# Attention with sigmoid and two mixture layers on one core: the last 64 keys of a head as a fourth, overlapping block, some weight splits on DVE alone, other pacing costs and a warm-up

## The chip, the cores and the metric

The kernel runs on one core of a Trainium2 chip. The metric is the device time of one execution in microseconds (us). Of the engines, TensorE (PE in the profile; PEld is its weight loads) multiplies matrices into PSUM, VectorE (DVE) and ScalarE (ACT) work element by element, GpSimd (POOL) issues the indirect transfers, and SyncE (SP) issues the other DMAs. Each engine runs its instructions in the order of the program; semaphores make it wait for the others.

## The reference

There are three stages, over 4 batches, 12 heads, 448 positions and 64 features a head, thus 1792 tokens of 768 features:

```python
scores = scale * np.matmul(q, k.transpose(0, 1, 3, 2)) - np.log(S)
attn = 1.0 / (1.0 + np.exp(-scores))
out = np.matmul(attn, v)                           # stage 1
x = out.transpose(0, 2, 1, 3).reshape(B * S, H * D)
h = np.maximum(np.maximum(x @ w1, x @ w2), x @ w3)
x = h @ w_out                                      # stage 2
logits = x @ w_gate + modality_bias[modality_id]   # stage 3: 8 experts, the best one per token
out[mask] = gate_w[mask, None] * (np.maximum(x[mask] @ w1[e], 0.0) @ w2[e])
```

The attention is a sigmoid of each score by itself; there is no sum over keys to divide by. The four weights of stage 2 (`w1`, `w2`, `w3`, `w_out`) come as 64-bit floats.

## The kernel before, in words

Most matmuls use a fast form of fp32 (`fp32r`). To keep the precision, an operand is split into a rounded part and the rest (`split`, line 172: ScalarE copies the rounded part, DVE subtracts it), and a product is made of three matmuls: rounded by rounded, rounded by rest, rest by rounded. Attention times values is in plain fp32.

**Attention** (lines 309 to 370). A unit is a pair of heads; there are 24. For a unit, SP loads queries and keys (`load_qk`), and values (`load_v`), three or four units ahead; `split_qk` (line 250) makes the rounded part and the rest on ScalarE and DVE. `emit_qk` (line 266) makes the scores: 448 keys are three blocks of 128 and a rest of 64. A full block takes 6 matmuls (three products, two heads side by side on 64 rows each; line 276). The rests of both heads are put together in one 128x128 weight tile, `k2`, that POOL fills and in which the other entries stay zero (lines 262 and 323), so they take three full matmuls (line 279). Each block's scores go to one of three PSUM buffers in turn (line 270), and a sigmoid on ScalarE (line 284) moves them to SBUF. `emit_av` multiplies by the values: line 296 for a full block, line 299 for the rests, in two tiles of 64x64. `evac_X` (line 301) splits the result out of PSUM into `xR` and `xL`, on DVE alone.

The order of an iteration, by hand, is: scores and sigmoids of unit u+1 (behind its first block: the loads, and the split of unit u+2), attention times values of unit u, its evacuation, and then a piece of `background` work.

**Background work** (lines 212 to 238). The weights of stage 2 arrive in 24 chunks. A chunk takes one load on SP, six conversion steps on DVE (64-bit to 32-bit float, `cv_ops`, lines 161 to 169) and, for the 18 chunks that are not of `w_out`, a `split` into one of four places of a ring (lines 173 and 174). These are entries of a queue, `bg`, each with a cost in us that is written down by hand; `background(us)` takes entries until their written costs have used up the budget:

```python
while us > 0 and (bg or bg2):
    ...
    if bg and (bg[0][2] is None or bg[0][2] in used):
        op, cost, _ = bg.popleft()
    elif bg2 and loaded[0] > LAST_O and step[0] >= bg2[0][2]:
        op, cost, _ = bg2.popleft()
    else:
        return
    op()
    us -= cost
```

The first queue goes ahead; an entry that would overwrite a ring place still to be used blocks it, and then the second one, `bg2`, has its turn. In attention, from unit 3 on, the budget is 1.2 a unit, until the chunk (1, 0), the fourth of the ring, is ready.

**Projection** (lines 414 to 440). 36 calls of `project`, "projects" 0 to 35: six blocks of 128 features, two halves of the tokens, three weights. Each has 36 matmuls (line 423) into one of two PSUM buffers. The first weight's result is copied by ScalarE (line 427), and the other two are joined to it with a maximum on DVE (line 429). Behind each project stands a "slot", `background(5.4)`. Beside the chunks, the slots make the gate weights: the product of `w_out` and `w_gate` (`bg2`, lines 393 to 412), in three tables of 48 operations each on DVE (line 402). A table is asked for by a DMA (line 399), and its operations may come only two projects later. Line 407 sums up the three, and line 440 empties both queues behind the last slot.

**After it.** The logits (line 447) are made from the maxima and the gate weights, ahead of everything else on TensorE. Then `w_out` and the maxima are split (lines 459 to 472), and `layer2` (line 487) follows with the routing of the tokens beside it, and then the experts.

Of the kernel before, what the change touches and what calls it, by code (L numbers as in the profile page):

```python
# [23 lines left out]
E64_LO = float(np.uint32(0x38000000).view(np.float32))  # L24
E64_HI = float(np.uint32(0x47EFFFFF).view(np.float32))
# [3 lines left out]
def attn_moe_kernel(  # L29
# [15 lines left out]
    nc = tc.nc  # L45
    B, HP, D, _, _, S = qk.shape
# [3 lines left out]
    FB = FF // 128  # L50
    NU = B * HP
    NJ = S // 128
    NB = 2 * NJ + 1
    SR = S - 128 * NJ
    TT = NT // 128
    GT = 256
# [7 lines left out]
    XW = DM + 16  # L64
    qscale = 1.0 / float(D) ** 0.5
    ln_s = float(np.log(S))

# [5 lines left out]
    def hold(tag, name, *shape):  # L75
        return pool.tile([128, *shape], F32, tag=tag, name=name)

    def r(ap):
        return ap.bitcast(F32R)

    def cut(a, off, *shape):

        n = 1
        for s in shape:
            n *= s
        a = a[:, off:off + n]
        if len(shape) == 2:
            a = a.rearrange("p (a b) -> p a b", a=shape[0])
        elif len(shape) == 3:
            a = a.rearrange("p (a b c) -> p a b c", a=shape[0], b=shape[1])  # L90
        return a
# [5 lines left out]
    xR = [xR_[:, i] for i in range(KB)]  # L97
    xL = [xLa[:, i] for i in range(KB - 1)] + [xLb[:, 0]]

    at_ = hold("H1", "at", 2 * NB * S + NB * D)  # L100
    atb = [cut(at_, NB * S * i, NB, S) for i in range(2)]

    kq_ = hold("H2", "kq", 8 * S)
    kq = [cut(kq_, 4 * S * i, 2, 2, S) for i in range(2)]

    k2_ = hold("K1", "k2", 2, 2, 128)
    k2 = [k2_[:, i] for i in range(2)]
    u1, u2, u3 = (hold(f"U{i}", f"u{i}", 2048) for i in range(3))
    qk_in = [cut(u, 2 * S * i, 2, S) for u in (u1, u2) for i in range(2)]
    v_in = [cut(u3, NB * D * i, NB, D) for i in range(4)] + [cut(at_, 2 * NB * S, NB, D)]  # L110

    stage = [hold(f"S{i}", f"stage{i}", KB * 256).bitcast(I32) for i in range(2)]
    cv_ = hold("S2", "cv", 2, 768)
# [31 lines left out]
    def ps(tag, shape, name):  # L145
        return psum.tile(shape, F32, tag=tag, name=name)
# [5 lines left out]
        return psum.tile(shape, F32, tag=f"a{a_n[0]}", name=name)  # L152


    def cv_ops(i, dst):
        st = stage[i % 2].rearrange("p (n two) -> p n two", two=2)
        lo, hi = st[:, :, 0], st[:, :, 1]
        v1, v2 = cv1, cv2
        ve = nc.vector
        return [  # L160
            lambda: ve.tensor_scalar(out=v1.bitcast(I32), in0=hi, scalar1=0x7FFFFFFF, scalar2=None, op0=ALU.bitwise_and),
            lambda: ve.tensor_scalar(out=v1, in0=v1, scalar1=E64_LO, scalar2=E64_HI, op0=ALU.max, op1=ALU.min),
            lambda: ve.tensor_scalar(out=v1.bitcast(I32), in0=v1.bitcast(I32), scalar1=0x0FFFFFFF, scalar2=3,
                                     op0=ALU.bitwise_and, op1=ALU.logical_shift_left),
            lambda: ve.scalar_tensor_tensor(out=v1.bitcast(U32), in0=lo.bitcast(U32), scalar=29, in1=v1.bitcast(U32),
                                            op0=ALU.logical_shift_right, op1=ALU.bitwise_or),
            lambda: ve.tensor_scalar(out=v2.bitcast(U32), in0=hi.bitcast(U32), scalar1=-0x80000000, scalar2=0x40000000,
                                     op0=ALU.bitwise_and, op1=ALU.bitwise_xor),
            lambda: ve.tensor_tensor(out=dst().bitcast(U32), in0=v1.bitcast(U32), in1=v2.bitcast(U32), op=ALU.bitwise_xor),  # L169
        ]  # L170

    def split(dR, dL, src):
        nc.scalar.activation(out=r(dR), in_=src, func=ACTF.Copy)  # L173
        nc.vector.tensor_tensor(out=r(dL), in0=src, in1=dR, op=ALU.subtract)  # L174

    ws = [w.bitcast(I32) for w in (w1, w2, w3)]
# [6 lines left out]
    def flat(a):  # L183
        return a.rearrange("p a b -> p (a b)")
# [28 lines left out]
    for i, (kind, a, b) in enumerate(chunks):  # L213
        bg.append((load_chunk, 0.0, None))
        ops = cv_ops(i, (lambda: cv1) if kind == "w" else (lambda a=a: wof[a]))
        bg.extend((op, 0.65, None) for op in ops)
        if kind == "w":
            m = w_ring[ring_no[a, b]]
            old = [c for c in ring_no if ring_no[c] == ring_no[a, b] and c < (a, b)]
            bg.append((lambda m=m, c=(a, b): (split(flat(m[:, 0]), flat(m[:, 1]), cv1), ready.add(c)), 0.85,  # L220
                       old[-1] if old else None))
    bg2 = deque()
    step = [0]
    ready = set()
# [16 lines left out]
    def load_qk(u):  # L241
        b, hp = divmod(u, HP)
        for h in range(2):
            nc.sync.dma_start(out=qk_in[u % 4][D * h:D * (h + 1)], in_=qk[b, hp, :, h])

    def load_v(u):
        b, hp = divmod(u, HP)
        nc.sync.dma_start(out=v_in[u % 5], in_=v[b, hp])

    def split_qk(u):  # L250
        src, kt = qk_in[u % 4], kq[u % 2]
        if u == 0:
            nc.vector.tensor_copy(out=r(kt[:, 0, 0]), in_=src[:, 0])
            nc.scalar.activation(out=r(kt[:, 0, 1]), in_=src[:, 1], func=ACTF.Copy)  # L254
            for i in range(2):
                nc.vector.tensor_tensor(out=r(kt[:, 1, i]), in0=src[:, i], in1=kt[:, 0, i], op=ALU.subtract)
        else:
            nc.scalar.activation(out=r(kt[:, 0]), in_=src, func=ACTF.Copy)
            nc.vector.tensor_tensor(out=r(kt[:, 1]), in0=src, in1=kt[:, 0], op=ALU.subtract)
        for h in range(2):  # L260
            p = slice(D * h, D * (h + 1))
            nc.gpsimd.tensor_copy(out=r(k2[u % 2][p, :, SR * h:SR * (h + 1)]), in_=kt[p, :, 0, 128 * NJ:])

    s_n = [0]

    def emit_qk(u, g):


        kt = kq[u % 2]
        s = ps(("a0", "a1", "t")[s_n[0] % 3], [128, 2, 512], "s")  # L270
        s_n[0] += 1
        for n, (a, x) in enumerate(((0, 0), (0, 1), (1, 0))):
            if g < NJ:
                for h in range(2):
                    p = slice(D * h, D * (h + 1))
                    nc.tensor.matmul(s[:, h, 0:S], r(kt[p, a, 0, 128 * g:128 * (g + 1)]), r(kt[p, x, 1]),  # L276
                                     start=(n == 0), stop=(n == 2))
            else:
                nc.tensor.matmul(s[:, 0, 0:S], r(k2[u % 2][:, a]), r(kt[:, x, 1]), start=(n == 0), stop=(n == 2))  # L279
        return s  # L280

    def emit_sig(u, g, s):
        n = 2 if g < NJ else 1
        nc.scalar.activation(out=atb[u % 2][:, 2 * g:2 * g + n], in_=s[:, 0:n, 0:S],  # L284
                             func=ACTF.Sigmoid, scale=qscale, bias=nlns)

    X_t = {}
# [1 line left out]
    def emit_av(u, g):  # L289
        if g == 0:  # L290
            X_t[u] = ps(f"x{u % 2}", [128, 512], "X")
        vt, at = v_in[u % 5], atb[u % 2]
        for h in range(2):
            dst = X_t[u][64 * h:64 * h + 64, 0:S]
            if g < NJ:
                nc.tensor.matmul(dst, vt[:, 2 * g + h], at[:, 2 * g + h], start=(g == 0), stop=False)  # L296
            else:
                p = slice(SR * h, SR * (h + 1))
                nc.tensor.matmul(dst, vt[p, 2 * NJ], at[p, 2 * NJ], start=False, stop=True)  # L299

    def evac_X(u):
        b, hp = divmod(u, HP)
# [5 lines left out]

    with tc.manual_schedule(engines={mybir.EngineType.PE, mybir.EngineType.Activation, mybir.EngineType.DVE, SP}):
        load_qk(0)  # L310
        make_identity(nc, ident)
        nc.vector.memset(nlns, -ln_s)
        nc.scalar.activation(out=gate[:, 0:1], in_=nlns, func=ACTF.Sigmoid)
# [3 lines left out]
        load_v(1)  # L317
        load_qk(3)
        load_v(2)
        nc.vector.memset(gw, 0.0)  # L320
        nc.vector.memset(ones, 1.0)
        for i in range(2):
            nc.vector.tensor_copy(out=r(k2[i]), in_=gw.rearrange("p a b -> p (a b)")[:, 0:1].unsqueeze(1).to_broadcast([128, 2, 128]))

        nc.gpsimd.memset(tri, 1.0)
        nc.gpsimd.affine_select(out=tri, in_=tri, pattern=[[1, 128]], compare_op=ALU.is_gt, fill=0.0,
# [81 lines left out]

        for c in range(3):
            bg2.append((lambda c=c: gate_load(c), 0.0, 0))  # L410
            bg2.extend((lambda c=c, kb=kb, e=e: gate_op(c, kb, e), 0.47, 100 + c) for kb in range(KB) for e in range(E))
        bg2.append((gate_end, 0.2, 0))

        def project(fb, half, wi):
# [18 lines left out]
        for fb in range(KB):  # L433
            for half in range(2):
                for wi in range(3):
                    project(fb, half, wi)
                    step[0] += 1
                    background(5.4)
        step[0] += 100
        background(999)  # L440

# [526 lines left out]
```

## Time and profile before

| | |
|---|---|
| time, median of 3 runs | 806.4 us (804.61 to 807.2) |
| time of the profiled execution | 807.21 us |
| its span | 805.5 us |
| TensorE (PE), busy | 780.2 us, 97% |
| weight loads (PEld) | 650.2 us, 81% |
| DVE | 484.9 us, 60% |
| ScalarE (ACT) | 283.3 us, 35% |
| GpSimd (POOL) | 79.2 us, 10% |
| DMA | 88.02 MB, mean 109 GB/s |

How to read it: the span runs from the first to the last instruction that the profile holds, and the execution's own time is 1.7 us longer. Busy shares are averages over all stages. By the chain of work that ended last, attention takes the first 164 us, the projection goes to 430, and the expert layers begin at some 537 and fill most of the rest. In a timeline a line is: start, duration, engine, line of the kernel, operation, what it writes and reads, shapes, how many were merged into the line, and in brackets how long the engine sat idle before it and what ended that. The records of neighbouring matmuls overlap, as they are pipelined.

### The profile page before, as it was taken

To read this page: it belongs to the slowest core of one execution; us is meant where nothing else is said; L and a number is where in the kernel's file an instruction comes from. 1 tells how busy PE (TensorE), PEld (TensorE's weight loads), DVE (VectorE), ACT (ScalarE), POOL (GpSimd) and SP (SyncE) were. 2 spreads that over 40 slices of the span, in tenths; PEclk is the share of its full clock that TensorE was granted. 3 is DMA by queue.
4 is the path that set the end of the run, shared out by engine and by line. 5 is a ranking of instruction groups with operands and counts; after the bars stand their busy time and mean duration, and the time that the engine had idled before them with its cause. 6 is when DMAs were issued, how large, how long until landed. Compare 5 with 4: busy or idle time off the path is not lost.

```text
span 805.5 us, 12040 instructions
## 1 busy us (share of the span) xinstructions
PE 780.2 (97%) x4660; PEld 650.2 (81%) x4660; DVE 484.9 (60%) x919; ACT 283.3 (35%) x401; POOL 79.2 (10%) x130
## 2 busy tenths in 40 slices
PE   6998998999999999999999999999999999999994
PEld 4444454489999999999987888898999999899993
DVE  2455553367949996999955822246555465556532
ACT  5676666501001010101004223235544455454522
POOL 2010000000000000000010060120220302021000
PEclk9999999999999999999999999999999999999997
DMA  9655473014433022201000195243657401064000
GB/s 237 173 144 144 118 153 95 1 40 129 146 131 118 1 70 100 79 1 52 1 1 1 62 380 222 93 145 141 246 171 264 158 17 64 14 235 157 23 25 17
DMA packets 42130, 88.02 MB, mean 109 GB/s; under 512 B 6067, under 2 KB 24756, under 8 KB 41686
## 3 DMA queue, kind: packets, MB, share of 16 engines
q1 hardware_dynamic: 38502, 75.68, 29.3%
q0 software_dynamic: 3568, 11.54, 4.3%
q8 instruction: 38, 0.62, 0.3%
q14 instruction: 22, 0.18, 0.1%
HBM read 94.93 MB, written 11.54 MB: 132 GB/s over the span
## 4 chain that ended last, share of the span: by engine, by line
PE 80%; DVE 12%; issue 3%; DMA 2%; ACT 0%; POOL 0%; SPq 0%; POOLq 0%; ACTq 0%; DVEq 0%
PE acc L423 21%; PE oacc L760 15%; PE hacc L739 14%; DVE gk L402 8%; PE X L296 7%; PE acc L487 7%; PE s L276 6%; PE X L299 3%; PE acc2b L487 3%; PE s L279 3%; PE xT L700 1%; DMA xg<-x2d,idx 1%; DVE hB L429 1%; DVE cv L169 1%; PE lgp L447 1%
## 5 line engine op out<-in xcount | busy, mean ns | idle before, releaser
L423 PE MATMUL acc<-xR,w_ring 128*128 128x448 f32 x864 | 210.9, 365 | 1.8 <-DVE hB L429 1.8
L423 PEld LDWEIGHTS acc<-xR,w_ring 128*128 128x128 f32 x864 | 162.4, 188 | 16.0 <-DVE hB L429 2.4
L760 PE MATMUL oacc<-wo_ck,xh 128*128 128x512 f32 (+1 forms) x672 | 124.0, 340 | 0.0
L739 PE MATMUL hacc<-xh,wo_ck 128*128 128x256 f32 x1008 | 122.3, 283 | 0.0
L739 PEld LDWEIGHTS hacc<-xh,wo_ck 128*128 128x128 f32 x1008 | 121.9, 192 | 0.3
L760 PEld LDWEIGHTS oacc<-wo_ck,xh 128*128 128x128 f32 x672 | 102.8, 188 | 13.7
L423 PE MATMUL acc<-xLa,w_ring 128*128 128x448 f32 x360 | 102.9, 367 | 0.0
L402 DVE SCALAR_TENSOR_TENSOR gk<-wof,gk 128x256 f32<-128x256 f32 x144 | 96.2, 668 | 4.3
L284 ACT ACTIVATE at<-s,nlns 128x896 f32<-128x896 f32 x96 | 82.5, 915 | 42.2 <-PE s L276 41.6
L174 DVE TENSOR_TENSOR wo_ck<-raw,wo_ck 128x512 fp32r<-128x512 f32 (+1 forms) x108 | 75.5, 744 | 6.0 <-ACT wo_ck L173 5.8
L487 PE MATMUL acc<-wo_ck,hs 128*128 128x512 f32 x252 | 78.7, 398 | 0.0
L423 PEld LDWEIGHTS acc<-xLa,w_ring 128*128 128x128 f32 x360 | 68.0, 189 | 5.5
L173 ACT ACTIVATE wo_ck<-raw 128x512 fp32r<-128x512 f32 (+1 forms) x108 | 67.0, 671 | 11.6 <-PE hacc L739 11.4
L276 PEld LDWEIGHTS s<-kq 64*128 64x128 f32 x432 | 40.1, 191 | 25.4 <-issue 14.1
L276 PE MATMUL s<-kq 64*128 64x448 f32 x432 | 52.5, 385 | 6.1 <-ACT kq L254 5.9
L487 PEld LDWEIGHTS acc<-wo_ck,hs 128*128 128x128 f32 x252 | 47.3, 188 | 12.2 <-ACT wo_ck L173 0.8
L487 PE MATMUL acc2b<-wo_ck,hs 128*128 128x256 f32 x252 | 56.2, 280 | 0.0
L306 DVE CAST xR<-X 128x448 fp32r<-128x448 f32 x24 | 15.0, 625 | 61.1 <-PE X L299 61.1
L296 PE MATMUL X<-at,u 128*64 128x448 f32 x240 | 51.2, 563 | 0.0
L427 ACT ACTIVATE hA<-acc 128x896 f32<-128x896 f32 x8 | 7.4, 922 | 111.6 <-PE acc L423 111.6
L746 DVE SCALAR_TENSOR_TENSOR xh<-hacc,xh 128x1024 fp32r<-128x1024 f32 x14 | 17.1, 1225 | 46.3 <-ACT xh L745 46.3
L691 POOL DMA_INDIRECT xg<-x2d,idx x30 | 29.5, 983 | 150.6 <-PE xT L700 101.1
(175 smaller groups left out, 737.8 us busy)
## 6 DMA issues: line engine op xcount, KB each, us to landing
raw<-in_moe_w_dram SPq DMA_DIRECT2D x24, 1024.0 KB
stage<-in_moe_w_dram SPq DMA_DIRECT2D x18, 768.0 KB
u<-in_qk_dram SPq DMA_DIRECT2D x48, 224.0 KB
raw<-in_moe_w_dram SPq DMA_DIRECT2D x12, 768.0 KB
raw_S<-in_moe_w_dram SPq DMA_DIRECT2D x12, 768.0 KB
stage<-in_moe_w_out_dram SPq DMA_DIRECT2D x6, 768.0 KB
u<-in_v_dram SPq DMA_DIRECT2D x20, 224.0 KB
x2d<-xo SPq DMA_DIRECT2D x14, 256.0 KB
```

Source lines behind the costliest of these rows:

```text
L173: nc.scalar.activation(out=r(dR), in_=src, func=ACTF.Copy)
L174: nc.vector.tensor_tensor(out=r(dL), in0=src, in1=dR, op=ALU.subtract)
L276: nc.tensor.matmul(s[:, h, 0:S], r(kt[p, a, 0, 128 * g:128 * (g + 1)]), r(kt[p, x, 1]), start=(n == 0), stop=(n == 2))
L279: nc.tensor.matmul(s[:, 0, 0:S], r(k2[u % 2][:, a]), r(kt[:, x, 1]), start=(n == 0), stop=(n == 2))
L284: nc.scalar.activation(out=atb[u % 2][:, 2 * g:2 * g + n], in_=s[:, 0:n, 0:S], func=ACTF.Sigmoid, scale=qscale, bias=nlns)
L296: nc.tensor.matmul(dst, vt[:, 2 * g + h], at[:, 2 * g + h], start=(g == 0), stop=False)
L402: nc.vector.scalar_tensor_tensor(out=junk, in0=wof[kb][:, GD * c:GD * (c + 1)], scalar=1.0, in1=wgb.rearrange("p (d e) -> p d e", e=E)[:, ...
L423: nc.tensor.matmul(acc[:, c, 0:S], r(m[:, a, kk, :]), r(x[kk][:, c0 + S * c:c0 + S * (c + 1)]), start=(kk == 0 and n == 0), stop=(kk == KB ...
L487: nc.tensor.matmul(acc_t[t, c], r(hs[t][:, a, kk, :]), r(wo_rl[c][:, kk, b]), start=(kk == 0 and n == 0), stop=(kk == KB - 1 and n == 2))
L691: nc.gpsimd.indirect_dma_start(out=xg[i % 2][s][:, XC[c][0]:XC[c][1]], out_offset=None, in_=x2d[c], in_offset=bass.IndirectOffsetOnAxis(ap ...
L739: nc.tensor.matmul(acc[:, f], r(w[a][:, 128 * f:128 * (f + 1)]), r(x[:, kk]), start=(kk == 0 and m == 0 and f % 2 == 0), stop=(kk == KB - ...
L760: nc.tensor.matmul(dst, r(x[:, f, 128 * s:128 * (s + 1)]), r(w[a][:, c0:c1]), start=(f == 0 and m == 0 and not (shared and s == 1)), stop= ...
```

## The change

- The last keys of each head become a fourth block of 128 keys, number 320 to 447, which overlaps the third by 64. The values of the 64 keys that it repeats are zeros: five value buffers get them once, by POOL's memset at the start, and `load_v` writes only the other 64 rows, with a second DMA. The scores have four blocks of 6 matmuls, the sigmoids are all 128x896, and attention times values is four blocks in one form. `k2` goes, with POOL's copies. The fifth value buffer moves to a place of its own.
- `split_qk` makes its rounded part on DVE instead of ScalarE. The weight splits of the first four ring chunks, made beside attention, are on DVE alone.
- The written costs: 0.58 or 0.97 a conversion step instead of 0.65; 0.97 a split (1.55 on DVE alone) instead of 0.85; 0.78 a gate operation instead of 0.47. The budget of a slot is 6.0 instead of 5.4; that of a unit stays at 1.2.
- Ten matmuls on a tile of zeros (`gw`) go to TensorE at the start, and their two memsets on DVE come first.

```diff
-    NB = 2 * NJ + 1
+    NB = 2 * (NJ + 1)
+    WARM = 10
...
+    v_in = [cut(u3, NB * D * i, NB, D) for i in range(4)] + [hold("K1", "v4", NB, D)]
...
+    US_1, US_2, US_SUM = 0.58, 0.97, 0.78
     def cv_ops(i, dst):
...
-    def split(dR, dL, src):
-        nc.scalar.activation(out=r(dR), in_=src, func=ACTF.Copy)
+    def split(dR, dL, src, alone=False):
+        if alone:
+            nc.vector.tensor_copy(out=r(dR), in_=src)
+        else:
+            nc.scalar.activation(out=r(dR), in_=src, func=ACTF.Copy)
         nc.vector.tensor_tensor(out=r(dL), in0=src, in1=dR, op=ALU.subtract)
...
-        bg.extend((op, 0.65, None) for op in ops)
+        bg.extend((op, cost, None) for op, cost in ops)
...
+            first = len(ring_no) and (a, b) <= (1, 0)
+            bg.append((lambda m=m, c=(a, b), first=first: (split(flat(m[:, 0]), flat(m[:, 1]), cv1, first), ready.add(c)),
+                       US_2 + US_1 * first, old[-1] if old else None))
...
     def load_v(u):
-        nc.sync.dma_start(out=v_in[u % 5], in_=v[b, hp])
+        nc.sync.dma_start(out=v_in[u % 5][:, 0:2 * NJ], in_=v[b, hp, :, 0:2 * NJ])
+        nc.sync.dma_start(out=v_in[u % 5][128 - SR:128, 2 * NJ:NB], in_=v[b, hp, :, 2 * NJ].rearrange("(h p) d -> p h d", h=2))
...
-            nc.scalar.activation(out=r(kt[:, 0]), in_=src, func=ACTF.Copy)
+            nc.vector.tensor_copy(out=r(kt[:, 0]), in_=src)
             nc.vector.tensor_tensor(out=r(kt[:, 1]), in0=src, in1=kt[:, 0], op=ALU.subtract)
-        for h in range(2):
-            p = slice(D * h, D * (h + 1))
-            nc.gpsimd.tensor_copy(out=r(k2[u % 2][p, :, SR * h:SR * (h + 1)]), in_=kt[p, :, 0, 128 * NJ:])
...
     def emit_qk(u, g):
+        k0 = min(128 * g, S - 128)
         s = ps(("a0", "a1", "t")[s_n[0] % 3], [128, 2, 512], "s")
...
+                nc.tensor.matmul(s[:, h, 0:S], r(kt[p, a, 0, k0:k0 + 128]), r(kt[p, x, 1]), start=(n == 0), stop=(n == 2))
...
+            nc.tensor.matmul(dst, vt[:, 2 * g + h], at[:, 2 * g + h], start=(g == 0), stop=(g == NJ))
...
         load_qk(0)
+        nc.vector.memset(gw, 0.0)
+        nc.vector.memset(ones, 1.0)
+        for vt in v_in:
+            nc.gpsimd.memset(vt[0:128 - SR, 2 * NJ:NB], 0.0)
         make_identity(nc, ident)
...
+        warm = ps("x1", [128, 512], "warm")
+        for i in range(WARM):
+            nc.tensor.matmul(warm[:, 0:KB * 32], ones, gw.rearrange("p a b -> p (a b)"), start=True, stop=True)
...
-            bg2.extend((lambda c=c, kb=kb, e=e: gate_op(c, kb, e), 0.47, 100 + c) for kb in range(KB) for e in range(E))
+            bg2.extend((lambda c=c, kb=kb, e=e: gate_op(c, kb, e), US_SUM, 100 + c) for kb in range(KB) for e in range(E))
...
-                    background(5.4)
+                    background(6.0)
```

## Rows read from the trace of the kernel before

**Rows 1.** Timeline, one unit of attention (start us, us, engine, what)
```profile
18.03 2.09 PE L276 MATMUL s<-kq 64*128 64x448 f32 x18
...
19.00 1.01 ACT L284 ACTIVATE at<-s,nlns 128x896 f32<-128x896 f32 x1 [2.04 <-PE s L276]
...
20.13 0.50 PEld L279 LDWEIGHTS s<-kq,k 128*128 128x128 f32 x3 [0.39 <-issue]
...
20.88 1.09 DVE L259 TENSOR_TENSOR kq<-u,kq 128x896 fp32r<-128x896 f32 x1 [1.46 <-ACT kq L258]
...
20.94 2.48 PE L296 MATMUL X<-at,u 128*64 128x448 f32 x12
21.37 0.14 PEld L296 LDWEIGHTS X<-at,u 128*64 128x64 f32 x2 [0.23 <-issue]
21.75 0.14 PEld L296 LDWEIGHTS X<-at,u 128*64 128x64 f32 x2 [0.23 <-issue]
...
23.35 0.97 PE L299 MATMUL X<-at,u 64*64 64x448 f32 x4
24.25 0.67 PE L276 MATMUL s<-kq 64*128 64x448 f32 x4
```

**Rows 2.** Timeline, the unit with the first break in attention
```profile
75.29 0.95 DVE L169 TENSOR_TENSOR cv<-cv 128x768 uint32<-128x768 uint32 x1
76.27 0.84 ACT L173 ACTIVATE w_ring<-cv 128x768 fp32r<-128x768 f32 x1 [3.37 <-DVE cv L169]
...
78.15 0.85 PE L279 MATMUL s<-kq,k 128*128 128x448 f32 x3 [2.09 <-ACT at L284]
```

**Rows 3.** Timeline, first matmuls of the unit with the second break and of the next
```profile
119.52 2.09 PE L276 MATMUL s<-kq 64*128 64x448 f32 x18
...
129.49 2.09 PE L276 MATMUL s<-kq 64*128 64x448 f32 x18
```

**Rows 4.** Timeline of ACT, projection: the copies behind projects 0 and 30
```profile
171.54 0.92 ACT L427 ACTIVATE hA<-acc 128x896 f32<-128x896 f32 x1 [12.86 <-PE acc L423]
...
390.00 0.92 ACT L427 ACTIVATE hB<-acc 128x896 f32<-128x896 f32 x1 [12.76 <-PE acc L423]
```

**Rows 5.** Timeline of PE, late in the projection
```profile
413.69 0.68 PE L423 MATMUL acc<-xR,w_ring 128*128 128x448 f32 x2 [1.81 <-DVE hB L429]
```

**Rows 6.** Busy time by stretch, behind that wait (us, each engine's busy time, clock, DMA)
```profile
413.69:418.60 4.91, 4.91 (x17) 4.41 (x18) 1.49 (x5) 0.00 (x0) 0.44 (x1) 0.65 0.02 4
```

**Rows 7.** Timeline of DVE, projection: first and last of 12 gate operations
```profile
318.21 0.67 DVE L402 SCALAR_TENSOR_TENSOR gk<-wof,gk 128x256 f32<-128x256 f32 x1
...
326.07 0.69 DVE L402 SCALAR_TENSOR_TENSOR gk<-wof,gk 128x256 f32<-128x256 f32 x1
```

**Rows 8.** Timeline of DVE, the sum of the gate weights
```profile
414.94 0.30 DVE L407 TENSOR_REDUCE gw<-gk 128x48 f32<-128x144 f32 x1
```

**Rows 9.** Timeline, end of the projection
```profile
430.01 3.21 PE L447 MATMUL lgp<-hA,gw 128*32 128x512 f32 x29
...
430.11 1.09 DVE L429 TENSOR_TENSOR hB<-hB,acc 128x896 f32<-128x896 f32 x1 [6.12 <-PE acc L423]
```

**Rows 10.** Timeline, the kernel's start
```profile
1.15 0.17 DVE L321 MEMSET ones<- 128x128 f32 x1
...
3.35 0.59 SPq L248 DMA_DIRECT2D u<-in_v_dram  x1
...
6.89 3.35 PE L276 MATMUL s<-kq 64*128 64x448 f32 x16 [0.29 <-DVE kq L256]
```

**Rows 11.** Timeline, fp32 matmuls of the last expert tile
```profile
775.34 10.88 PE L892 MATMUL hacc<-ht,raw 128*128 128x128 f32 x96
```

**Rows 12.** Groups of instructions by shape, 20 to 160 us (count, busy us, mean ns, idle before)
```profile
L306 DVE CAST xR<-X 128x448 fp32r<-128x448 f32 x21 | 13.1, 625 | 51.8 <-PE X L299 51.8
...
L174 DVE TENSOR_TENSOR w_ring<-cv,w_ring 128x768 fp32r<-128x768 f32 x4 | 3.8, 952 | 1.8 <-ACT w_ring L173 1.8
...
L161 DVE TENSOR_SCALAR cv<-stage 128x768 int32<-128x768 int32 x4 | 2.2, 555 | 0.1
```

More of the change, by code (lines that the diff above doesn't have):

```diff
@@ L98, in attn_moe_kernel @@
     xL = [xLa[:, i] for i in range(KB - 1)] + [xLb[:, 0]]
-    at_ = hold("H1", "at", 2 * NB * S + NB * D)
+    at_ = hold("H1", "at", 2 * NB * S)
     atb = [cut(at_, NB * S * i, NB, S) for i in range(2)]
@@ L104, in attn_moe_kernel @@
     kq = [cut(kq_, 4 * S * i, 2, 2, S) for i in range(2)]
-    k2_ = hold("K1", "k2", 2, 2, 128)
-    k2 = [k2_[:, i] for i in range(2)]
     u1, u2, u3 = (hold(f"U{i}", f"u{i}", 2048) for i in range(3))
     qk_in = [cut(u, 2 * S * i, 2, S) for u in (u1, u2) for i in range(2)]
-    v_in = [cut(u3, NB * D * i, NB, D) for i in range(4)] + [cut(at_, 2 * NB * S, NB, D)]
+    v_in = [cut(u3, NB * D * i, NB, D) for i in range(4)] + [hold("K1", "v4", NB, D)]
     stage = [hold(f"S{i}", f"stage{i}", KB * 256).bitcast(I32) for i in range(2)]
@@ L160, in cv_ops @@
         return [
[L161 to L166, printed above, removed]
@@ L167, in cv_ops @@
-            lambda: ve.tensor_scalar(out=v2.bitcast(U32), in0=hi.bitcast(U32), scalar1=-0x80000000, scalar2=0x40000000,
-                                     op0=ALU.bitwise_and, op1=ALU.bitwise_xor),
-            lambda: ve.tensor_tensor(out=dst().bitcast(U32), in0=v1.bitcast(U32), in1=v2.bitcast(U32), op=ALU.bitwise_xor),
-        ]
-    def split(dR, dL, src):
-        nc.scalar.activation(out=r(dR), in_=src, func=ACTF.Copy)
+            (lambda: ve.tensor_scalar(out=v1.bitcast(I32), in0=hi, scalar1=0x7FFFFFFF, scalar2=None, op0=ALU.bitwise_and), US_1),
@@ new lines, in cv_ops @@
+            (lambda: ve.tensor_scalar(out=v1, in0=v1, scalar1=E64_LO, scalar2=E64_HI, op0=ALU.max, op1=ALU.min), US_1),
+            (lambda: ve.tensor_scalar(out=v1.bitcast(I32), in0=v1.bitcast(I32), scalar1=0x0FFFFFFF, scalar2=3,
+                                      op0=ALU.bitwise_and, op1=ALU.logical_shift_left), US_1),
+            (lambda: ve.scalar_tensor_tensor(out=v1.bitcast(U32), in0=lo.bitcast(U32), scalar=29, in1=v1.bitcast(U32),
+                                             op0=ALU.logical_shift_right, op1=ALU.bitwise_or), US_2),
@@ new lines, in cv_ops @@
+            (lambda: ve.tensor_scalar(out=v2.bitcast(U32), in0=hi.bitcast(U32), scalar1=-0x80000000, scalar2=0x40000000,
+                                      op0=ALU.bitwise_and, op1=ALU.bitwise_xor), US_1),
+            (lambda: ve.tensor_tensor(out=dst().bitcast(U32), in0=v1.bitcast(U32), in1=v2.bitcast(U32), op=ALU.bitwise_xor), US_2),
+        ]
+    def split(dR, dL, src, alone=False):
[3 more added lines that the diff above has]
+            nc.scalar.activation(out=r(dR), in_=src, func=ACTF.Copy)
@@ L219, in attn_moe_kernel @@
             old = [c for c in ring_no if ring_no[c] == ring_no[a, b] and c < (a, b)]
-            bg.append((lambda m=m, c=(a, b): (split(flat(m[:, 0]), flat(m[:, 1]), cv1), ready.add(c)), 0.85,
-                       old[-1] if old else None))
+            first = len(ring_no) and (a, b) <= (1, 0)
+            bg.append((lambda m=m, c=(a, b), first=first: (split(flat(m[:, 0]), flat(m[:, 1]), cv1, first), ready.add(c)),
+                       US_2 + US_1 * first, old[-1] if old else None))
     bg2 = deque()
@@ L272, in emit_qk @@
         for n, (a, x) in enumerate(((0, 0), (0, 1), (1, 0))):
[L273 to L279, printed above, removed]
+            for h in range(2):
+                p = slice(D * h, D * (h + 1))
+                nc.tensor.matmul(s[:, h, 0:S], r(kt[p, a, 0, k0:k0 + 128]), r(kt[p, x, 1]), start=(n == 0), stop=(n == 2))
         return s
     def emit_sig(u, g, s):
-        n = 2 if g < NJ else 1
-        nc.scalar.activation(out=atb[u % 2][:, 2 * g:2 * g + n], in_=s[:, 0:n, 0:S],
+        nc.scalar.activation(out=atb[u % 2][:, 2 * g:2 * g + 2], in_=s[:, :, 0:S],
                              func=ACTF.Sigmoid, scale=qscale, bias=nlns)
@@ L294, in emit_av @@
             dst = X_t[u][64 * h:64 * h + 64, 0:S]
[L295 to L299, printed above, removed]
+            nc.tensor.matmul(dst, vt[:, 2 * g + h], at[:, 2 * g + h], start=(g == 0), stop=(g == NJ))
     def evac_X(u):
@@ L319, in attn_moe_kernel @@
         load_v(2)
[L320 to L323, printed above, removed]
+        warm = ps("x1", [128, 512], "warm")
+        for i in range(WARM):
+            nc.tensor.matmul(warm[:, 0:KB * 32], ones, gw.rearrange("p a b -> p (a b)"), start=True, stop=True)
         nc.gpsimd.memset(tri, 1.0)
```

## The prediction

> **What bounds the kernel now.** I read the page first: in its first part TensorE is busy for 97% of the span. That is an average over stages, so I went on to the timeline, stage by stage.
>
> In attention (to 163.9 us) one unit, a pair of heads, takes 6.22 us, 18.03 to 24.25 [rows 1]: scores of three key blocks, scores of the last 64 keys (line 279), attention times values for three blocks (line 296), then for the last keys (line 299). TensorE goes from one to the next with short gaps only. Two things are to be seen. Where the form of the matmuls changes (128x64 to 64x64, say) the next one begins later than within a form: the value groups are 0.38 us apart (21.37, 21.75), so the six of line 296 are through at 20.94 + 6 x 0.38 = 23.22, and line 299 starts at 23.35. And the fourth block's scores go into the PSUM buffer of the first, whose sigmoid runs from 19.00 to 20.01; the weight load of line 279 begins at 20.13.
>
> Attention has two breaks. In the first, ScalarE's copy for a weight split waits 3.37 us for DVE, with a sigmoid queued behind it, and TensorE idles 2.09 us before 78.15 [rows 2]. The second is the same and lasts longer, as the matmuls run slowly after it: 119.52 to 129.49 is 9.97 us for one unit [rows 3], 3.75 too many. Together 5.8 us.
>
> In the projection (36 projects of 36 matmuls, lines 414 to 438) the first copy of an accumulator starts at 171.54, the one 30 projects later at 390.00: 7.28 us each [rows 4]. At that pace the last result would be ready at 171.54 + 35 x 7.28 = 426.4; its maximum on DVE starts at 430.11 [rows 9]. So 3.7 us are lost: DVE is behind, TensorE idles 1.81 us before 413.69 [rows 5] and then runs for 4.9 us at a mean granted clock of 0.65, so mostly at 1.2 GHz in place of 2.4, which costs 4.9 x 0.35 = 1.7 [rows 6].
>
> The gate weights (144 operations of line 402) are DVE filler in that stage. They start 0.714 us apart (318.21 to 326.07 for 11) [rows 7] and are through at 414.94 [rows 8], so the logits (line 447, the first matmuls behind the projection) start at 430.01 without a wait [rows 9].
>
> **The change, part by part.** Attention's scores: 24 matmuls of one form in place of 18 and 3. Today the fourth block's load comes 2.10 us after the unit's first matmul. The buffer of block one is free when its sigmoid ends, 1.98 after that matmul, and a load follows a semaphore by about 0.1 [rows 1]: it can't begin earlier than now, and three pairs behind it cost what three full matmuls cost. Gain 0; the other end, 0.2 us a unit, is a rival. The Trainium skill's page "TensorEngine Tiling (Array Packing)", section Key Properties, says that a change of the tiling mode drains the engine; by that rule alone the fourth block would follow at once, and the kernel would come out some 4.6 us lower.
>
> Values: a fourth block's group would start at 23.22, its second at 23.60; line 299's second starts at 23.35 + 0.38, and the unit ends 0.52 behind that. So the next unit starts at 24.12, not 24.25: 0.13 x 24 = **-3.1** (bounds 0.1 and 0.2: -2.4 to -4.8). The zero rows cost nothing: line 296 with 128 rows and line 299 with 64 are equally fast.
>
> ScalarE gets 448 columns more in the fourth sigmoid and loses the query/key copy; it idles 2.04 us before each first sigmoid [rows 1], so this is free. DVE takes the copies. Its worst unit has two evacuations of 0.62, the sixth conversion step 0.95, a weight copy 0.56 (as line 161), a subtraction 0.95 (line 174), the query/key copy about 0.65 (an estimate: a sixth more columns than line 161), a subtraction 1.09 [rows 1, 2, 12]: 5.4 of some 6.1 us. It fits; if it didn't, four such units would pay under 0.5 each (+2 at most). As ScalarE waits for DVE no more, both breaks go: **-5.8** (bounds -4 to -5.8). POOL's copies (line 262) go; at 0 (-0.5 at best, in the first unit). The last keys' values become a second transfer, one more issue on SP's queue, ahead of the query/key loads behind it. One value load's issue takes 0.59 at the start [rows 10], and everything lands units ahead of its use later: 0, at worst +0.6. POOL's five memsets stand ahead of the identity, which nothing needs for a long time: 0.
>
> Start: ten warm-up matmuls of 192 fp32 columns. By line 892 (96 records of 128 columns in 10.88 us, two records a matmul [rows 11]) they take 10 x 2 x 0.113 x 1.5 = 3.4 us at full clock, twice that at half. They need the memset that ends at 1.32 [rows 10], so from 1.4 they end between 4.8 and 8.2; I take 7.1, nearer the slow end, since the kernel's first matmuls run slowly today too. The scores of unit 0 now start at 6.89 and run at half pace: 8 pairs in 3.35 us [rows 10] where 9 take 2.09 later [rows 1], so 1.5 lost, and line 279's three behind them 0.5 more. Of these 2.0 I take off 0.2 for the later start and 0.2 for the sigmoids, 1.01 us each, which then set the pace: **-1.6** (0 if the warm-up ends at 8.2 with the clock still low, -2.5 at best).
>
> Projection: the steps are now costed nearer to their time (0.78 for a gate operation of 0.714), and a slot behind a project gets 6.0. Eight gate operations and a maximum are 5.7 + 1.0 = 6.7 of 7.28 us. DVE keeps up, and the loss comes back: **-3.7** (bounds -3.3 to -3.9).
>
> **But the filler isn't through.** I walked the queue by its written costs, which needs no times. With the old costs the walk puts the last gate operations and line 407 behind the maximum of project 32, three projects before the end, and that is where the trace has them, at 414.94 [rows 8]. With the new ones, slots 0 to 7 hold conversions and slot 8 nothing (a table has just been asked for, and its operations wait two projects). First table: one each in slots 9 to 11, 8 each in 12 to 14, one each in 15 to 17, then 8, 8 and 2 (48). Second: none, 1, 1, in 24 to 26 8 each, then 1, 7, 8, 6 (48, slot 30). Slot 31 is empty. Third: 8 each in 32 to 34. So 24 stand **behind the last maximum**: 8 in slot 35, 16 in the final drain. Behind them line 407, and for it the logits wait, which are next in TensorE's order: nothing can go ahead of them. TensorE waits for the maximum, 1.01, for 24 x 0.714 = 17.15, for line 407, 0.30, and a semaphore, 0.1: **+18.6** (18.3 to 18.8) [rows 7 to 9]. The output-weight splits queued behind this on DVE stay hidden: ScalarE makes its halves meanwhile, and DVE's run beside the logits.
>
> After that wait the clock will be low. Price: 1.7 after an idle time of 1.81 [rows 6], 2.0 at the kernel's start [rows 10]; after a long idle time the start is nearest: **+2.0** (0 to 3.5).
>
> Later stages are shifted whole. Sum: -3.1 - 5.8 - 1.6 - 3.7 + 18.6 + 2.0 = +6.4 us. The profiled run took 807.2 (span 805.5), 0.8 above the median of 806.4, so 813.6 by its own time and **812.8** by the median. A measurement of this kernel can tell some 0.3% (2.4 us) from no change.
>
> **Rivals.**
> (a) The fourth scores follow at once, since only the change of form delays their load today. For it: drain and sigmoid end within 0.02 us of each other in the trace, so it shows only that neither is later. Against: three buffers go round, and the fourth block must take the first's. Gain 0.2 x 23 = 4.6: 808.2, within 0.3%. Chance 0.11.
> (b) Faster: fewer gate operations stand behind the last maximum than I counted. Place: TensorE's wait before line 447, 0.714 an operation. At 15 in place of 24 loss and gain are even, at 11 it is faster by over 0.3%; with none, and no slow clock, 812.8 - 18.6 - 2.0 = 792.2. For it: today the queue is empty three projects early. Against: the count depends on nothing that a run changes, and the old one is in the trace. Chance 0.07.
> (c) Slower still: DVE, with all of attention's splits, is late for the next unit's scores, the warm-up holds up the first ones, and the clock stays low for longer: +2, +1.6 and +1.5 give 817.9. Chance 0.08.
> The forecast has 0.74.
>
> **Numbers.** Low end: rival (a) less 0.7 for the values' bound, 807.5; high end: (c), 818. Outside is (b) and the edges of (a) and (c), 0.15 in all. Slower: 0.74 + 0.08, less 0.03 for forecasts that end under 808.8: 0.79; same 0.14; faster 0.07.
>
> **What would show it.** Right: units of about 6.1 us, no breaks as at 78 and 122, attention over near 153; no wait of TensorE for a maximum; 24 gate operations behind the last maximum, and logits 18.6 us after the last project. Units of 5.9 show (a). Gate weights reduced before the last maximum show (b), and the prediction would be wrong.

## The result, and the profile after

The changed kernel takes 812.05 us (median of 4 runs, 811.67 to 812.66) beside 806.55 of the kernel before: a ratio of 1.0073, 95% interval 1.0054 to 1.0092. The forecast was 812.8. The profiled execution took 811.67, its span 810.0, against 807.21 and 805.5: 4.5 us more by the two traces, 5.5 by the medians; single runs of one kernel lie 1 to 2.6 us apart. One run of e7 below took 2712.6 us, for a reason that nothing here shows, and is left out of that kernel's median.

One unit of attention in the timeline of the changed kernel (start us, us, engine, what), to be held against [rows 1]:

```profile
77.05 2.91 PE L277 MATMUL s<-kq 64*128 64x448 f32 x24
...
78.03 3.70 ACT L281 ACTIVATE at<-s,nlns 128x896 f32<-128x896 f32 x4 [2.30 <-PE s L277]
...
79.09 0.50 PEld L277 LDWEIGHTS s<-kq 64*128 64x128 f32 x6 [0.32 <-ACT at L281]
...
79.89 3.23 PE L292 MATMUL X<-at,u 128*64 128x448 f32 x16
...
83.05 2.91 PE L277 MATMUL s<-kq 64*128 64x448 f32 x24
```

A unit takes 6.00 us (77.05 to 83.05) where it took 6.22. The weight loads of the fourth block pause 0.32 us and are released by ScalarE's sigmoid: the form no longer changes there, and the buffer's wait stands in the same place, 2.04 us after the unit's start instead of 2.10. The values, 79.89 to 83.05, take 3.16 instead of 3.31. The weight splits fall at other places than before. Their copies, now on DVE, start at 49.05, 67.35, 85.35 and 103.35; the third is this line:

```profile
85.35 0.56 DVE L174 CAST w_ring<-cv 128x768 fp32r<-128x768 f32 x1
```

The four units with a split begin at 46.74, 65.05, 83.05 and 101.05 and take 6.00 us each, so there is no break as in [rows 2]. One other unit takes 6.32 us (52.74 to 59.06): its first sigmoid starts 0.3 us late, after ScalarE has idled 2.60 us where it is 2.30 in the others. It doesn't wait for DVE; what held it the profile doesn't say.

The copies behind projects 0 and 30, as in [rows 4]:

```profile
159.98 0.92 ACT L424 ACTIVATE hA<-acc 128x896 f32<-128x896 f32 x1 [12.25 <-PE acc L420]
...
378.04 0.92 ACT L424 ACTIVATE hB<-acc 128x896 f32<-128x896 f32 x1 [13.99 <-PE acc L420]
```

Attention is over 11.6 us earlier (159.98 against 171.54), and the pace is 218.06 / 30 = 7.27 us a project, without a stop.

The end of the projection, against [rows 7 to 9]: the last maximum, first and last of the 24 gate operations behind it, their sum, the logits, and the first matmul of layer 2.

```profile
414.44 1.09 DVE L426 TENSOR_TENSOR hB<-hB,acc 128x896 f32<-128x896 f32 x1 [0.52 <-PE acc L420]
...
415.44 0.61 DVE L399 SCALAR_TENSOR_TENSOR gk<-wof,gk 128x256 f32<-128x256 f32 x1
...
430.67 0.62 DVE L399 SCALAR_TENSOR_TENSOR gk<-wof,gk 128x256 f32<-128x256 f32 x1
431.33 0.30 DVE L404 TENSOR_REDUCE gw<-gk 128x48 f32<-128x144 f32 x1
...
431.69 5.51 PE L444 MATMUL lgp<-hA,gw 128*32 128x512 f32 x29 [17.29 <-DVE gw L404]
...
439.28 0.50 PE L484 MATMUL acc<-wo_ck,hs 128*128 128x512 f32 x1
```

The last maximum now comes at 414.44 and not 430.11, and yet layer 2 starts at 439.28, later than at 435.29 before:

```profile
435.29 0.50 PE L487 MATMUL acc<-wo_ck,hs 128*128 128x512 f32 x1
```

TensorE stands still for 17.29 us, and then the logits take 7.59 us to layer 2 where they took 5.28 (430.01 to 435.29 before). The busy times of these two stretches show why (us, then busy time and count of PE, PEld, DVE, ACT and POOL, then granted clock and DMA):

```profile
414.00:431.70 17.70, 0.41 (x4) 0.04 (x3) 16.43 (x51) 5.89 (x14) 0.00 (x0) 0.65 0.00 0
431.70:439.28 7.58, 7.58 (x49) 1.99 (x49) 7.43 (x16) 0.00 (x0) 0.00 (x0) 0.69 0.00 0
```

In the first line only DVE is busy throughout (third pair, 16.43 of 17.70), ScalarE through with its part after 5.89. In the second the mean granted clock is 0.69, so 1.2 GHz in place of 2.4 for most of it: 7.58 x 0.31 = 2.3 us.

### The profile page after: what moved, and what is told of

Its sections match the earlier page's. It is cut to its first block, busy times and chain, and to the rows that moved or that the text cites. A ratio compares the mean times of both kernels' runs of the same rounds, so it can differ in the third digit from the quotient of the medians.

```text
span 810.0 us, 12155 instructions
## 1 busy us (share of the span) xinstructions
PE 778.3 (96%) x4752; PEld 655.2 (81%) x4752; DVE 499.3 (62%) x944; ACT 269.5 (33%) x374; POOL 65.3 (8%) x87
## 4 chain that ended last, share of the span: by engine, by line
PE 92%; issue 3%; DVE 2%; DMA 1%; POOL 0%; ACT 0%; POOLq 0%; DVEq 0%; ACTq 0%
PE acc L420 32%; PE oacc L757 15%; PE hacc L736 14%; PE X L292 9%; PE s L277 8%; PE acc L484 7%; PE acc2b L484 3%; DVE gk L399 2%; PE xT L697 1%; PE lgp L444 1%; DMA xg<-x2d,idx 1%; PE warm L320 1%; DMA x2d<-xo 0%; PE hacc L889 0%; POOL xg L688 0%
## 5 line engine op out<-in xcount | busy, mean ns | idle before, releaser
L281 ACT ACTIVATE at<-s,nlns 128x896 f32<-128x896 f32 x96 | 88.8, 1011 | 53.1 <-PE s L277 53.1
L420 PE MATMUL acc<-xLa,w_ring 128*128 128x448 f32 x360 | 101.2, 362 | 0.0
L277 PEld LDWEIGHTS s<-kq 64*128 64x128 f32 x576 | 50.2, 184 | 27.8 <-issue 15.7
L176 ACT ACTIVATE wo_ck<-raw 128x512 fp32r<-128x512 f32 (+1 forms) x108 | 67.0, 671 | 11.6 <-PE hacc L736 11.4
L277 PE MATMUL s<-kq 64*128 64x448 f32 x576 | 70.5, 380 | 0.3 <-ACT at L281 0.2
L292 PE MATMUL X<-at,u 128*64 128x448 f32 x320 | 64.3, 545 | 0.0
L292 PEld LDWEIGHTS X<-at,u 128*64 128x64 f32 x320 | 21.3, 136 | 34.1 <-issue 32.0
```

The source lines that it names most:

```text
L277: nc.tensor.matmul(s[:, h, 0:S], r(kt[p, a, 0, k0:k0 + 128]), r(kt[p, x, 1]), start=(n == 0), stop=(n == 2))
L281: nc.scalar.activation(out=atb[u % 2][:, 2 * g:2 * g + 2], in_=s[:, :, 0:S], func=ACTF.Sigmoid, scale=qscale, bias=nlns)
L420: nc.tensor.matmul(acc[:, c, 0:S], r(m[:, a, kk, :]), r(x[kk][:, c0 + S * c:c0 + S * (c + 1)]), start=(kk == 0 and n == 0), stop=(kk == KB ...
```

## The experiments

Eleven experiments were run, in this order. Times are medians, and ratios are to the kernel before on the same chip.

**No gate operation behind the last maximum (e1).**

```diff
-    US_1, US_2, US_SUM = 0.58, 0.97, 0.78
+    US_1, US_2, US_SUM = 0.58, 0.97, 0.714
...
-                    background(6.0)
+                    background(6.5)
```

> The changed kernel with a gate operation written at 0.714 instead of 0.78 and a slot's budget at 6.5 instead of 6.0, so that no gate operation stands behind the last maximum (24 in the changed kernel). My theory (the logits wait for those 24): the wait of 17.3 us and the slow 2.3 us behind it go, 812.05 - 19.6 = 792.4, between 791 and 795, as DVE may run up to 2 us late here and there. Rival (the wait is only moved: DVE's splits of the output weights, 8 us behind the last maximum, then hold layer 2): about 798 to 800. Rival (the loss is in attention, from the splits that DVE took over): no gain, 812.

Measured: 792.96 us against 806.09, a ratio of 0.9839 (0.9823 to 0.9856). Its timeline at the same place:

```profile
414.74 0.30 DVE L404 TENSOR_REDUCE gw<-gk 128x48 f32<-128x144 f32 x1
414.96 1.08 DVE L426 TENSOR_TENSOR hB<-hB,acc 128x896 f32<-128x896 f32 x1
...
415.10 3.21 PE L444 MATMUL lgp<-hA,gw 128*32 128x512 f32 x29 [1.12 <-DVE gw L404]
...
420.38 0.50 PE L484 MATMUL acc<-wo_ck,hs 128*128 128x512 f32 x1
```

Now the sum stands ahead of the last maximum. DVE comes to it some 0.9 us late, TensorE waits 1.12, and layer 2 starts at 420.38, again 5.28 us behind the logits. Both rivals fall: attention was no loss, and the output weights' splits behind the last maximum don't take over. This kernel beats both of the given ones.

**Half of the tail (e2).** The changed kernel with one number other:

```diff
-                    background(6.0)
+                    background(6.3)
```

> The changed kernel with a slot's budget of 6.3 instead of 6.0 and nothing else: 12 gate operations behind the last maximum instead of 24. My theory: 12 x 0.66 = 7.9 us less wait, the slow clock behind it as before: 804.1, between 803 and 805.5. If the wait's length didn't matter and only its being there (the clock): about 812. If the whole loss were another: 812 too.

Measured: 803.75 us, ratio 0.997 (0.9958 to 0.9983).

```profile
414.34 1.08 DVE L426 TENSOR_TENSOR hB<-hB,acc 128x896 f32<-128x896 f32 x1
...
423.30 0.30 DVE L404 TENSOR_REDUCE gw<-gk 128x48 f32<-128x144 f32 x1
...
423.66 5.93 PE L444 MATMUL lgp<-hA,gw 128*32 128x512 f32 x29 [9.44 <-DVE gw L404]
```

12 operations fewer, 17.29 - 9.44 = 7.85 us less wait, 0.654 each. The wait is a count of operations, as the walk through the queue has it.

**The new costs alone (e3).** The kernel before with the change's written costs and its budget of 6.0, everything else as it was:

```diff
+    US_1, US_2, US_SUM = 0.58, 0.97, 0.78
...
-        bg.extend((op, 0.65, None) for op in ops)
+        bg.extend((op, cost, None) for op, cost in zip(ops, (US_1, US_1, US_1, US_2, US_1, US_2)))
...
-            bg.append((lambda m=m, c=(a, b): (split(flat(m[:, 0]), flat(m[:, 1]), cv1), ready.add(c)), 0.85,
+            bg.append((lambda m=m, c=(a, b): (split(flat(m[:, 0]), flat(m[:, 1]), cv1), ready.add(c)), US_2,
...
-            bg2.extend((lambda c=c, kb=kb, e=e: gate_op(c, kb, e), 0.47, 100 + c) for kb in range(KB) for e in range(E))
+            bg2.extend((lambda c=c, kb=kb, e=e: gate_op(c, kb, e), US_SUM, 100 + c) for kb in range(KB) for e in range(E))
...
-                    background(5.4)
+                    background(6.0)
```

> The kernel before with the new written costs and the new budget of 6.0 alone; attention, splits on ScalarE and start as before. My theory: the projection's 4.1 us come back, and 24 gate operations stand behind the last maximum: 806.5 - 4.1 + 17.3 + 2.3 = 822.0, between 820 and 824. Rival (the loss comes from the work that DVE took over from ScalarE, or from the fourth block): at or under 802.4, as the pacing then only helps.

Measured: 825.06 us, ratio 1.0239 (1.0222 to 1.0256); 3 us above what I expected. The waits (engine, line, for whom: us in total, times, longest) and the timeline:

```profile
PE s L280 <- ACT at L285: 8.4, 4, 2.1
```

```profile
173.00 0.92 ACT L428 ACTIVATE hA<-acc 128x896 f32<-128x896 f32 x1 [12.85 <-PE acc L424]
...
444.97 6.04 PE L448 MATMUL lgp<-hA,gw 128*32 128x512 f32 x29 [17.26 <-DVE gw L408]
...
453.08 0.50 PE L488 MATMUL acc<-wo_ck,hs 128*128 128x512 f32 x1
```

The wait before the logits is the same 17.26, so the rival falls. The projection's gain comes with the costs alone too: from the copy behind project 0 to the last maximum, at 427.75, it took 254.75 us, 3.8 less than the 258.57 before. What I had left out: with the new costs all four weight splits beside attention come where a sigmoid waits behind them, four breaks of 2.1 us instead of two, and attention ends 1.5 us later than before (173.00 against 171.54). The logits took 8.11 us to layer 2, 0.5 more than in the changed kernel. These and the 0.3 that the projection gave back less make 2.3 of the 3 us; the rest is the sum's own, as I added terms from a trace of 807.2 us to a median of 806.5.

**No warm-up (e4).**

```diff
-    WARM = 10
+    WARM = 0
```

> The changed kernel without its ten warm-up matmuls. My theory: the scores of unit 0 run at half pace again, and the values of unit 0 start 1 to 1.3 us later: 813.2, between 812.5 and 814. Rival (the warm-up holds up the first scores by as much as the clock gives back): 812.0 or below.

Measured: 811.70 us (ratio 1.0071, 1.0055 to 1.0088) against 812.05 with the warm-up, so no loss; here the expectation was wrong. First the start with the warm-up (the changed kernel), then two stretches without it:

```profile
13.60 3.23 PE L292 MATMUL X<-at,u 128*64 128x448 f32 x16
16.75 2.90 PE L277 MATMUL s<-kq 64*128 64x448 f32 x24
```

```profile
6.94 7.41 PE L277 MATMUL s<-kq 64*128 64x448 f32 x46 [0.28 <-DVE kq L261]
...
14.29 3.23 PE L292 MATMUL X<-at,u 128*64 128x448 f32 x16
```

```profile
432.39 4.62 PE L444 MATMUL lgp<-hA,gw 128*32 128x512 f32 x29 [17.28 <-DVE gw L404]
...
439.09 0.50 PE L484 MATMUL acc<-wo_ck,hs 128*128 128x512 f32 x1
```

The values of unit 0 do start later, at 14.29 and not 13.60, and so does all else up to the logits (432.39, not 431.69). In this run the logits then took 6.70 us and not 7.59, as the clock rose earlier behind the wait (a mean granted clock of 0.78 in that stretch, not 0.69), and layer 2 starts no later. That is one trace of each kernel.

**The weight splits back on ScalarE (e5), the query/key copy back on ScalarE (e6).** Both by one line, from e1:

```diff
-            bg.append((lambda m=m, c=(a, b), first=first: (split(flat(m[:, 0]), flat(m[:, 1]), cv1, first), ready.add(c)),
+            bg.append((lambda m=m, c=(a, b), first=first: (split(flat(m[:, 0]), flat(m[:, 1]), cv1), ready.add(c)),
```

```diff
-            nc.vector.tensor_copy(out=r(kt[:, 0]), in_=src)
+            nc.scalar.activation(out=r(kt[:, 0]), in_=src, func=ACTF.Copy)
```

> e1_drained with the first four weight splits back on ScalarE and DVE (the query/key split stays on DVE). My theory (a sigmoid queued behind a copy that waits for DVE): all four come at the end of a conversion and break the scores of their unit by some 2.1 us each, as the four breaks of e3_pacing_only did: 793.0 + 8.2 = 801.2, and up to 804 if the clock falls behind one or two of them. Rival (with the query/key copy gone ScalarE has the time, so the breaks would be gone anyway): 793.

> e1_drained with the rounded part of queries and keys back on ScalarE, the weight splits on DVE alone. My theory: nothing late depends on it, ScalarE has 2.3 us idle before a unit's first sigmoid: 793.0, within 1 us. Rival (ScalarE, now with four full sigmoids a unit, becomes late and the fourth block's buffer with it): 0.3 us a unit or more, 800 or above.

These two and the next two ran on another chip, on which the kernel before takes 813.0 us. There the stretch from layer 2 to the end takes 372.9 to 376.8 us in the four traces, against 370.1 to 371.4 in the nine others, so the times expected above don't hold there; I compare these kernels by stage. Measured: e5 805.47 (ratio 0.9906, 0.9886 to 0.9925), e6 797.26 (0.9803, 0.9784 to 0.9821). They differ by 8.2 us. The waits of e5 have the four breaks that were expected:

```profile
PE s L277 <- ACT at L281: 8.0, 4, 2.0
```

The copy behind project 0, first in e5, then in e6:

```profile
167.15 0.92 ACT L424 ACTIVATE hA<-acc 128x896 f32<-128x896 f32 x1 [11.97 <-PE acc L420]
```

```profile
159.49 0.92 ACT L424 ACTIVATE hA<-acc 128x896 f32<-128x896 f32 x1 [11.97 <-PE acc L420]
```

It starts at 167.15 in e5 and at 159.49 in e6, against 159.55 in e1. So in the attention the gain of DVE's share is all in the weight splits; the query/key copy may stay on either engine.

**A short first sigmoid (e7), the old blocks (e8).** e7 is e1 with the first block's sigmoid on 64 of 448 queries, the rest of that block zero: that part of the attention is left out.

```diff
-        nc.scalar.activation(out=atb[u % 2][:, 2 * g:2 * g + 2], in_=s[:, :, 0:S],
+        w = S if g else 64
+        nc.scalar.activation(out=atb[u % 2][:, 2 * g:2 * g + 2, 0:w], in_=s[:, :, 0:w],
```

e8 is the kernel before, with `k2`, POOL's copies and lines 276 to 299 as they were, and with e1's splits, warm-up, costs and budget.

> e1_drained with the first block's sigmoid cut to 64 of 448 queries of each head; the rest of that block stays zero, so this part of attention is left out. My theory (the fourth block's scores wait for the end of the first sigmoid, as their PSUM buffer is its own): the wait goes, the scores take 2.7 us instead of 2.84 and a unit some 5.8 to 5.85 instead of 6.0: 793.0 - 24 x 0.17 = 789, between 788 and 790. Rival (the pause before the fourth block is a drain of TensorE and has nothing to do with the sigmoid): 793, unit 6.0.

> The kernel before with everything of e1_drained but the fourth overlapping block: the last keys of both heads in one weight tile filled by POOL, as before, one value transfer; splits on DVE, warm-up and e1's pacing. My theory: the fourth block is worth 6.22 - 6.00 = 0.22 us a unit and no more: 793.0 + 24 x 0.22 = 798.2, between 797.5 and 799. Rival (the block form matters more, since POOL's copies now follow DVE, and the scores wait for them): 800 or above; rival (the gain of the blocks is only the splits' place): 793.

Measured: e7 791.35 us (0.9736, 0.9716 to 0.9755), e8 804.61 (0.9895, 0.9879 to 0.9912). A unit of e7:

```profile
79.83 2.74 PE L277 MATMUL s<-kq 64*128 64x448 f32 x24
80.81 0.37 ACT L282 ACTIVATE at<-s,nlns 128x128 f32<-128x128 f32 x1 [2.39 <-PE s L277]
...
82.49 0.20 PEld L293 LDWEIGHTS X<-at,u 128*64 128x64 f32 x4 [0.31 <-DMA u<-in_qk_dram]
...
85.65 0.69 PE L277 MATMUL s<-kq 64*128 64x448 f32 x4
```

The copy behind project 0, first in e7, then in e8:

```profile
154.65 0.92 ACT L427 ACTIVATE hA<-acc 128x896 f32<-128x896 f32 x1 [12.36 <-PE acc L423]
```

```profile
164.31 0.92 ACT L436 ACTIVATE hA<-acc 128x896 f32<-128x896 f32 x1 [13.13 <-issue]
```

With the sigmoid at 0.37 us nothing stands between the third block's scores and the fourth's: the 24 matmuls, up to the first weight load of the values, take 2.66 us (79.83 to 82.49) instead of 2.84, a unit 5.82. The copy behind project 0 comes 4.9 us earlier than in e1, at 154.65. So the pause in the changed kernel is the sigmoid, as the prediction has it; the rival, a drain of TensorE, falls. In e8 the units are 6.21 us again, and that copy comes at 164.31, 4.8 us later than in e1 (I expected 5.2). The fourth block by itself is worth 0.2 us a unit.

**TensorE kept busy through the wait (e9).** The changed kernel with 84 matmuls of no use behind the last project, into a PSUM buffer that is free then:

```diff
         background(999)
+        idle = ps("x1", [128, 512], "idle")
+        m = w_ring[ring_no[5, 0]]
+        for i in range(84):
+            nc.tensor.matmul(idle[:, 0:S], r(m[:, 0, i % KB, :]), r(xR[i % KB][:, 0:S]), start=True, stop=True)
```

> The changed kernel with 84 matmuls of no use (448 columns, 0.202 us each, 17.0 us in all) on TensorE between the last project and the logits, while DVE works through its 24 gate operations. My theory: the clock is not low when the logits start, they take 5.3 us and not 7.6, so 2.3 us are the clock's price; and the gate operations, 0.661 us apart while TensorE stood still, are 0.714 apart again, as they are beside the projection: 1.3 us more. In all 812.05 - 2.3 + 1.3 = 811.0. Rival (the gate operations' pace has another cause): still 0.66, and 809.7. Rival (the logits are slow for another reason than the clock): 7.6 us again, and 812 to 813.3.

Measured: 810.00 us against 806.38, a ratio of 1.0048 (1.0031 to 1.0065). The changed kernel has 1.0073 (1.0054 to 1.0092), so the total alone doesn't tell the two apart; the stage does.

```profile
413.68 17.15 PE L441 MATMUL idle<-xR,w_ring 128*128 128x448 f32 x84
...
429.19 0.66 DVE L399 SCALAR_TENSOR_TENSOR gk<-wof,gk 128x256 f32<-128x256 f32 x1
429.89 0.67 DVE L399 SCALAR_TENSOR_TENSOR gk<-wof,gk 128x256 f32<-128x256 f32 x1
430.61 0.62 DVE L399 SCALAR_TENSOR_TENSOR gk<-wof,gk 128x256 f32<-128x256 f32 x1
...
431.27 0.62 DVE L399 SCALAR_TENSOR_TENSOR gk<-wof,gk 128x256 f32<-128x256 f32 x1
```

```profile
432.30 3.20 PE L448 MATMUL lgp<-hA,gw 128*32 128x512 f32 x29 [1.47 <-DVE gw L404]
...
437.57 0.50 PE L488 MATMUL acc<-wo_ck,hs 128*128 128x512 f32 x1
```

The logits take 5.27 us to layer 2 (432.30 to 437.57) at a mean granted clock of 1.00, as in the kernel before: the 2.3 us were the clock's. And the gate operations are 0.67 us long beside the matmuls; they change to 0.62 at 430.61, as the matmuls come to their end at 430.83.

**e1 again, and without the warm-up (e10, e11).** e10 is e1; e11 is e1 with `WARM = 0`.

> The kernel of e1_drained once more, beside the kernel without its warm-up. My theory: the ratio to the kernel before is 0.984 again, as the shares that it is made of (attention 11.5 us, projection 4, less 1 us of wait) don't depend on the chip; where the stores between the layers take longer, both kernels do. Rival (a part of the gain was that chip's): 0.99 or above.

> e1_drained without its ten warm-up matmuls. My theory: 0.7 us slower than e1_drained, by the 0.7 us that unit 0's values start later without the warm-up in e4_no_warm (14.29 against 13.60), so at the edge of what the runs can tell. Rival (the first units wait for their sigmoids, and the warm-up gives nothing): no difference.

Measured: e10 793.66 us, ratio 0.9845 (0.9831 to 0.9859); e11 793.56, 0.9842 (0.9828 to 0.9855). The gain of e1 is there again; the warm-up gives nothing that can be measured. Where its share goes, the chain of waits shows between layer 2 and the experts; first e10, then e11:

```profile
503.94 0.98 POOL xg L688
...
505.22 5.25 DMA xg<-x2d,idx
```

```profile
505.02 0.96 POOL xg L688
...
506.29 4.19 DMA xg<-x2d,idx
```

Without the warm-up the gather of the first expert tile is asked for 1.08 us later, and its data land at the same time, 510.47 and 510.48. That this is where the share goes isn't shown: in e1, the kernel of e10, the same gather took 4.65 us and landed at 509.74. What sets its end was not tried.

## Why the prediction was right, step by step

| step | predicted, us | by the two traces | from |
|---|---|---|---|
| scores and values | -3.1 | -4.5 (with the unit of 6.32) | from the second iteration's scores to the copy behind project 0, less the breaks: 171.54 - 18.03 - 5.8 = 147.7; after, 159.98 - 16.75 = 143.2 |
| the two breaks | -5.8 | -5.8 | none left |
| start | -1.6 | -1.3 | those scores start at 16.75 instead of 18.03 |
| projection | -3.7 | -4.1 | copy behind project 0 to last maximum: 258.57 and 254.46 |
| wait before the logits | +18.6 | +17.3 | logits against the last maximum: 0.1 us before it, 17.25 behind it |
| low clock | +2.0 | +2.3 | logits to layer 2: 5.28 and 7.59 |
| the rest | 0 | +0.5 | layer 2 to the span's end: 370.21 and 370.72 |
| sum | +6.4 | +4.5 | |

The mechanism was right in each of its large terms. The sum is 1.9 us too high by the two traces, mostly by two terms that missed the same way: scores and values gained 1.4 more, and the tail cost 1.3 less. That 812.8 came within 0.8 us of the median is partly luck: the trace of before, from which the terms are taken, lies 0.7 us above the median to which they were added.

- **The tail** was counted rightly: 24 operations in the trace, all gain lost to them, shown from three sides (none, 12, and the costs put into the kernel before). The step that was mis-sized is its pace: I took 0.714 us an operation from the projection, and with TensorE at a standstill it is 0.662 (415.44 to 430.67 for 23): 1.3 us less.
- **The clock behind the wait** came within 0.3 us of the price that I took from the kernel's start, and e9 shows it as a quantity of its own. In the four traces with such a wait the logits took 6.7 to 8.1 us.
- **The fourth block's scores** are held by the first sigmoid (rival (a) falls with e7). But "gain 0" was a little too low: the fourth block's load comes 2.04 us after the unit's start and not 2.10. Before, the profile names no releaser for that load ("issue"), so that the change of form held it for the 0.06 us is likely, but no run shows it by itself. The values gave 0.15 instead of 0.13. Together 0.22 a unit, not 0.13. The Trainium skill's page "TensorEngine Tiling (Array Packing)", section Key Properties, has a change of the tiling mode drain the engine; e7, without a change and without the sigmoid's wait, shows 0.18 us less for the scores (2.66 against 2.84), and that is the size of what the rule could have given.
- **The breaks** went with the weight splits' copies and come back with them (e5, e3). With the new costs and the splits left on ScalarE there would have been four (e3, e5), not two; the prediction took the two that the old costs make. That DVE has room for all of attention's splits held: the scores never wait for DVE, and the one late unit has another cause. With that and the clock's 2.3 us rival (c) falls.
- **The start** is where the reasoning was weak, and that its term came out near is luck. The warm-up makes 0.7 of the 1.3 us: without it those scores start at 17.44 (e4) and not 16.75. The rest is the trace of before itself: in e3, with the same instructions up to there, they start at 17.24 and not 18.03. What the term had wrong is the sigmoids, for which I took off 0.2: in the changed kernel the weight loads of the fourth to the eighth block come 0.9 us apart (9.20, 10.10, 10.99, 11.89, 12.79), each released by a sigmoid. And the 0.7 can't be found at the end in e4 and e11; I had priced a gain at the start as if everything behind it moved with it.
- Rival (b), fewer operations in the tail than counted, is the kernel that one would have wanted: e1 is that case, at 793.0 where I had worked out 792.2.

## What to carry to other kernels

Work that is fed in by written costs has an end as well as a pace: walk the queue to its last entry before the costs or the budget are changed, and count what stands behind the last result that the next stage needs. Costs that are true for each operation can still leave a queue unfinished, if slots stay empty for other reasons (here a table's two-project delay); the budget has to make up for these. And of two waits that end together, removing one gives only the difference between them.

## What the runs showed of the hardware that I had not expected

DVE's gate operations (two SBUF inputs of 256 elements) take 0.62 us while TensorE stands still and 0.67 while it streams matmuls, 0.66 and 0.71 from start to start. e9 shows the step within one run, at the operation that starts at 430.61. ScalarE's work beside them ends by 420.4 in both kernels and changes neither figure. Which of TensorE's accesses they meet was not tried.

A start 0.8 us earlier was not to be found at the end: layer 2 starts at 420.52 with the warm-up (e10) and at 421.35 without (e11), and the medians are 793.66 and 793.56. From there to the end the nine traces that are not of e5 to e8 take 370.1 to 371.4 us, and the gather in it 4.2 to 5.3. One trace of each can't tell where the 0.8 us went; it stays open.
